# W3's last 64 features done behind W4's row tiles, with W4's sums split 256 and 384

## The chip, the cores and the metric

The kernel runs on one core of one Trainium2 chip. The metric is the device time of one launch in microseconds (us), of the slowest core, which here is the only one. A profile is one execution with every instruction recorded. PE is TensorE, PEld its weight loads, DVE VectorE, ACT ScalarE, SP the engine that issues most of the DMAs.

A timed run scatters by 1 us or more between executions. A trace is far steadier within its loop: the distance between two matmuls of the same program repeats to about 0.01 us. For an effect of some tenths of a us I therefore lean on distances inside the traces, and use the timed runs for the larger effects that I provoke on purpose.

## The reference, cut to what matters

The whole computation mixes a linear attention block and an MLP block over 2048 tokens of 640 features. The change touches only the last part of the MLP block:

```python
x1 = x + hs                                          # 2048 x 640
h2 = _gelu(_layernorm(x1, axis=-1) @ w3) @ w4         # w3: 640 x 1728, w4: 1728 x 640
b  = x1 + h2
return g * a + (1 - g) * b                            # a: attention block, g: gate per token
```

1728 is 13 chunks of 128 features and one rest of 64. That rest is what the change moves.

## The kernel before

The tokens are done in four tiles (`t` = 0 to 3) of 512 tokens (`TS`), each of four chunks of 128 (`cc`). PSUM, where the matmuls leave their sums, is handed out by the kernel in four "pairs" of two banks of 512 float32 columns, and there is no fifth pair.

The rest of 64 features uses the array in halves. In W3 only 64 of its 128 columns are needed, so two matmuls, each for half of the tile's tokens (`LT` = 256), run side by side: "column tiles", 128 rows by 64 columns. In W4 only 64 of its 128 rows are needed, so two matmuls for two chunks of tokens run side by side: "row tiles", 64 by 128. Everything else in this loop uses the array whole ("full").

```python
    def w3_unit(t, i):                       # two chunks of features into one PSUM pair
        ...                                  # cut: h2 and lnT (transposed LayerNorm) of the tile
        pt = pair()
        for k in range(2):
            fc = 2 * i + k
            if fc < FF:                      # FF = 13 full chunks
                for dc in range(DC):
                    nc.tensor.matmul(pt[:, k, :], lhsT=w3_sb[:, dc, fc * P:(fc + 1) * P], rhs=lnT[:, dc, :], ...)
            else:                            # the rest: column tiles
                for dc in range(DC):
                    for v in range(2):
                        nc.tensor.matmul(pt[FR * v:FR * (v + 1), k, 0:LT], lhsT=w3_sb[:, dc, FF * P:F],
                                         rhs=lnT[:, dc, v * LT:(v + 1) * LT], ...)
        ...                                  # cut: GELU on ScalarE, PSUM -> h2

    def w4_tile(t):
        pts = {cc: pair() for cc in (0, 2)}
        for cc in (0, 2):
            ...                              # cut: x1_scale of the next tile (ScalarE)
            for hf in range(2):              # two halves of the 640 outputs
                w4_mm(t, cc, pts, hf, True)  # 13 matmuls
        for cc in (1, 3):
            pts[cc] = pair()
        w4_rest(t, pts)                      # row tiles: end chunks 0 and 2, begin 1 and 3
        for cc in (0, 2):
            w4_out(t, cc, pts[cc])           # VectorE: * (1 - g) + x1, then the store
        last = t == NT - 1
        for cc, hf in ((3, 0), (1, 0), (1, 1), (3, 1)) if last else ((1, 0), (1, 1), (3, 0), (3, 1)):
            ...                              # cut
            w4_mm(t, cc, pts, hf, False)
            ...                              # cut: output of the piece

    for t in range(NT):                      # the loop
        for i in range(NW3):                 # 7 units of W3, with W2 of t + 1 and attention of t between them
            w3_unit(t, i)
            ...                              # cut: w2_unit(t + 1, i), att_unit(t, i - 2)
        if t + 1 < NT:
            ...                              # cut: ln2_rstd
            for cc in range(CPT):
                ln2_apply(t + 1, cc)         # LayerNorm of t + 1 and its DMA transpose into lnT
        w4_tile(t)
```

So in each tile PE goes from full to column tiles (end of W3), to full (W4's first half), to row tiles, and to full again (W4's second half): four changes of the array's shape.

## Time and profile before

| | before |
|---|---|
| time, median of the first 3 runs | 266.99 us (266.32 to 267.23) |
| span of the profile | 265.1 us |
| PE busy | 259.4 us, 98% |
| DVE, ACT, POOL busy | 53%, 32%, 8% |
| granted TensorE clock | 0.997 |

These are the first part of the page (busy us, share of the span, instructions) and the head of its fourth part (the chain of waits that ended last, by engine):

```profile
PE 259.4 (98%) x1728; PEld 162.0 (61%) x1744; DVE 139.3 (53%) x270; ACT 84.2 (32%) x122; POOL 20.3 (8%) x55
...
PE 95%; DMA 1%; ACT 1%; issue 0%; ACTq 0%; DVE 0%
```

PE sets the time. A busy PE is no proof of a full one, though: matmul records overlap (a 320-column matmul is recorded with 0.30 us but the next starts 0.136 us later), so a gap of 0.1 us between two groups is covered by the records and counts as busy. It shows only in the starts. This is PE's timeline of before at the end of W3 and through W4 in tile 1 (start, length, engine, line, operation, tile of the array, shape, how many):

```profile
168.69 1.24 PE L459 MATMUL pp<-lnxT,w_sb 128*128 128x512 bf16 x5
169.86 0.74 PE L464 MATMUL pp<-lnxT,w_sb 128*64 128x256 bf16 x10
170.53 7.24 PE L476 MATMUL pp<-w_sb,h 128*128 128x320 bf16 x52
177.70 0.72 PE L485 MATMUL pp<-w_sb,h 64*128 64x320 bf16 x8
178.35 0.45 PE L476 MATMUL pp<-w_sb,h 128*128 128x320 bf16 x2
```

L464 are the column tiles and L485 the row tiles. (Here and in later views the last line can be cut off by the window that was asked for: all 26 or 52 matmuls of W4 follow.) Five matmuls of 512 columns at the steady 0.216 us would end their stream at 169.77; the column tiles start at 169.86, 0.09 us later. Ten column tiles in pairs of 0.109 us take 0.55 us, to 170.41; W4 starts at 170.53, 0.12 us later. Fifty-two matmuls at 0.1358 us take 7.06 us, to 177.59; the row tiles start 0.11 us later. Four pairs of row tiles take 0.54 us; W4 goes on 0.11 us later. Each change of shape leaves about 0.1 us in which PE streams nothing.

The tail of before, DVE at the end of tile 3. L501 is the last arithmetic of the kernel, on the last 320 columns:

```profile
259.53 0.88 DVE L492 SCALAR_TENSOR_TENSOR oc<-pp,omg,x 128x640 bf16<-128x640 f32 x1 [2.32 <-PE pp L476]
261.29 0.55 DVE L501 SCALAR_TENSOR_TENSOR oc<-pp,omg,x 128x320 bf16<-128x320 f32 x1 [0.88 <-PE pp L476]
```

### The profile page before, as it was taken

To read this page: it belongs to the slowest core of one execution; us is meant where nothing else is said; L and a number is where in the kernel's file an instruction comes from. 1 tells how busy PE (TensorE), PEld (TensorE's weight loads), DVE (VectorE), ACT (ScalarE), POOL (GpSimd) and SP (SyncE) were. 2 spreads that over 40 slices of the span, in tenths; PEclk is the share of its full clock that TensorE was granted. 3 is DMA by queue.
4 is the path that set the end of the run, shared out by engine and by line. 5 is a ranking of instruction groups with operands and counts; after the bars stand their busy time and mean duration, and the time that the engine had idled before them with its cause. 6 is when DMAs were issued, how large, how long until landed. Compare 5 with 4: busy or idle time off the path is not lost.

```text
span 265.1 us, 4244 instructions
## 1 busy us (share of the span) xinstructions
PE 259.4 (98%) x1728; PEld 162.0 (61%) x1744; DVE 139.3 (53%) x270; ACT 84.2 (32%) x122; POOL 20.3 (8%) x55
## 2 busy tenths in 40 slices
PE   8999999999999999999999999999999999999994
PEld 4667555788755644565666556567556567455662
DVE  1688688899858588955422364512464503122032
ACT  1555544321165636522510313430212340333100
POOL 7100010012300140001000001000001000000000
PEclk9999999999999999999999999999999999999998
DMA  7999987015663527500132000132000042000011
GB/s 195 181 212 370 377 242 298 0 40 122 127 97 64 78 51 193 205 0 2 29 70 77 25 0 2 21 78 77 25 0 2 1 99 77 25 0 2 0 62 37
DMA packets 46092, 23.61 MB, mean 89 GB/s; under 512 B 35450, under 2 KB 45434, under 8 KB 46074
## 3 DMA queue, kind: packets, MB, share of 16 engines
q1 hardware_dynamic: 45632, 22.86, 33.2%
q10 hardware_dynamic: 442, 0.49, 0.5%
q8 instruction: 13, 0.21, 0.4%
q14 instruction: 5, 0.04, 0.1%
HBM read 12.21 MB, written 2.62 MB: 56 GB/s over the span
## 4 chain that ended last, share of the span: by engine, by line
PE 95%; DMA 1%; ACT 1%; issue 0%; ACTq 0%; DVE 0%
PE pp L476 22%; PE pp L459 21%; PE pp L307 8%; PE pp L412 8%; PE pp L443 8%; PE pp L190 8%; PE pp L341 8%; PE pp L232 8%; DMA wk_sb<-in_A_wqkv_dram 1%; PE pp L464 1%; PE pp L485 1%; ACT m_sb L381 1%; PE pp L360 1%; PE pp L247 0%; PE pp L379 0%
## 5 line engine op out<-in xcount | busy, mean ns | idle before, releaser
L467 ACT ACTIVATE h<-pp 128x1024 bf16<-128x1024 f32 (+1 forms) x28 | 27.8, 992 | 102.8 <-PE pp L459 94.4
L459 PE MATMUL pp<-lnxT,w_sb 128*128 128x512 bf16 x249 | 59.8, 379 | 0.6
L476 PE MATMUL pp<-w_sb,h 128*128 128x320 bf16 x416 | 57.9, 299 | 0.0
L476 PEld LDWEIGHTS <-h 128*128 128x128 bf16 x416 | 40.0, 98 | 17.0 <-issue 1.9
L459 PEld LDWEIGHTS <-w_sb 128*128 128x128 bf16 x260 | 25.4, 98 | 26.7
L492 DVE SCALAR_TENSOR_TENSOR oc<-pp,omg,x 128x640 bf16<-128x640 f32 x15 | 12.9, 882 | 44.1 <-PE pp L485 27.1
L446 DVE SCALAR_TENSOR_TENSOR x<-pp,gate,x 128x640 f32<-128x640 f32 x16 | 13.9, 868 | 29.4 <-PE pp L443 29.4
L415 DVE TENSOR_TENSOR x<-pp,x_sb 128x640 f32<-128x640 f32 x16 | 13.1, 820 | 22.6 <-PE pp L412 22.6
L182 ACT ACTIVATE e<-pp 128x640 bf16<-128x640 f32 (+1 forms) x26 | 21.5, 826 | 9.6 <-PE pp L232 9.6
L443 PE MATMUL pp<-m_sb,pqT 128*128 128x320 bf16 x160 | 24.3, 299 | 0.0
L412 PE MATMUL pp<-w_sb,hsT 128*128 128x320 bf16 x160 | 23.9, 299 | 0.1
L190 PE MATMUL pp<-wk_sb,xT 128*128 128x320 bf16 (+1 forms) x160 | 22.7, 300 | 0.1
L307 PE MATMUL pp<-x_sb,pk 128*128 128x320 bf16 (+1 forms) x160 | 22.3, 300 | 0.0
L232 PE MATMUL pp<-xT,hsT 128*128 128x512 bf16 x98 | 21.6, 379 | 0.1
L307 PEld LDWEIGHTS <-pk 128*128 128x128 bf16 x160 | 18.8, 117 | 3.5
L412 PEld LDWEIGHTS <-hsT 128*128 128x128 bf16 x160 | 15.6, 98 | 8.2 <-issue 0.2
L443 PEld LDWEIGHTS <-pqT 128*128 128x128 bf16 x160 | 15.7, 98 | 7.7
L190 PEld LDWEIGHTS <-xT 128*128 128x128 bf16 x160 | 15.4, 98 | 6.6 <-DMA xT<-in_A_x_dram 0.6
L341 PE MATMUL pp<-lnxT,w_sb 128*128 128x512 bf16 x77 | 17.8, 379 | 0.2
L232 PEld LDWEIGHTS <-hsT 128*128 128x128 bf16 x100 | 11.8, 118 | 9.7
L277 POOL TENSOR_SCALAR rstd<-mv 128x4 f32<-128x4 f32 (+1 forms) x11 | 3.4, 312 | 156.5 <-DVE mv L283 156.5
L184 DVE SCALAR_TENSOR_TENSOR pk<-pp,e 128x640 bf16<-128x640 f32 x16 | 13.2, 824 | 1.7
(76 smaller groups left out, 189.7 us busy)
## 6 DMA issues: line engine op xcount, KB each, us to landing
out_dram<-oc SPq DMA_DIRECT2D x15, 160.0 KB, 1.8
w_sb<-in_B_w_dram SPq DMA_DIRECT2D x1, 2160.0 KB, 8.4
w_sb<-in_B_w_dram SPq DMA_DIRECT2D x1, 2080.0 KB, 10.2
x_sb<-in_A_x_dram SPq DMA_DIRECT2D x2, 640.0 KB, 10.0
x_sb<-in_A_x_dram SPq DMA_DIRECT2D x1, 1120.0 KB, 7.5
wo_sb<-in_A_wo_dram SPq DMA_DIRECT2D x6, 160.0 KB, 7.7
hsT<-in_A_wqkv_dram SPq DMA_DIRECT2D x1, 800.0 KB, 5.0
m_sb<-in_A_wqkv_dram SPq DMA_DIRECT2D x1, 800.0 KB, 11.1
```

Of the source, the lines that this page charges most:

```text
L182: nc.scalar.activation(ev, src, ACT.Exp)
L184: nc.vector.scalar_tensor_tensor(dst, src, 0.0, ev, op0=ALU.max, op1=ALU.add)
L190: nc.tensor.matmul(pt[:, hf, 0:n], lhsT=xT[:, dc, c * P:(c + 1) * P], rhs=wk_sb[:, dc, hf * HD:hf * HD + n], start=(dc == 0), stop=(dc == ...
L232: nc.tensor.matmul(pt[:, t % 2, :], lhsT=wq_sb[:, dc, :].rearrange("p (m j) -> p j m", j=DC)[:, j], rhs=xT[:, dc, t * TS:(t + 1) * TS], st ...
L307: nc.tensor.matmul(pt[:, hf, 0:HD + hf], lhsT=w, rhs=x_sb[:, c, hf * HD:(hf + 1) * HD + hf], start=(c == 0), stop=(c == NCH - 1))
L341: nc.tensor.matmul(pt[:, i, :], lhsT=w, rhs=lnxT[t][:, dc, :], start=(dc == 0), stop=(dc == DC - 1))
L412: nc.tensor.matmul(pt[:, hf, 0:HD], lhsT=hsT[:, fc, 2 + c * P:2 + (c + 1) * P], rhs=w2_sb[:, fc, hf * HD:(hf + 1) * HD], start=(fc == 0), ...
L443: nc.tensor.matmul(pt[:, hf, 0:HD], lhsT=pqT[:, j, c * P:(c + 1) * P], rhs=m_sb[:, j, hf * HD:(hf + 1) * HD], start=(j == 0), stop=(j == D ...
L446: nc.vector.scalar_tensor_tensor(x1, pt[:, :, 0:HD], gate[:, c:c + 1], x1, op0=ALU.mult, op1=ALU.add)
L459: nc.tensor.matmul(pt[:, k, :], lhsT=w3_sb[:, dc, fc * P:(fc + 1) * P], rhs=lnT[:, dc, :], start=(dc == 0), stop=(dc == DC - 1))
L467: nc.scalar.activation(h2[:, 2 * i * TS:2 * i * TS + n], pt[:].rearrange("p h e -> p (h e)")[:, 0:n], ACT.Gelu_apprx_tanh)
L476: nc.tensor.matmul(dst, lhsT=st[t]["h2"][:, fc * TS + cc * P:fc * TS + (cc + 1) * P], rhs=w4_sb[:, fc, a:b], start=start and fc == 0, stop ...
```

## The change

The intent: do the column tiles of the *next* tile of tokens right behind the row tiles of this one, so that PE goes full, row, column, full, and the column tiles no longer need a visit of their own. They need PSUM columns for that, and all four pairs are taken by W4. So W4's 640 sums are cut into 256 and 384: 256 in the upper half of a pair's first bank and 384 in its second bank, which leaves 256 columns free in the first. In the last tile the pieces are put in an order that leaves a 256-column piece for last.

```diff
+    h2x_p = ctx.enter_context(tc.tile_pool(name="h2x_p", bufs=2))
 ...                                     # w3_unit: the else branch with the column tiles is gone
+    def w3_rest(t, dst):
+        for dc in range(DC):
+            for v in range(2):
+                nc.tensor.matmul(dst[FR * v:FR * (v + 1), :], lhsT=w3_sb[:, dc, FF * P:F],
+                                 rhs=st[t]["lnT"][:, dc, v * LT:(v + 1) * LT], start=(dc == 0), stop=(dc == DC - 1))
+        st[t]["h2x"] = h2x_p.tile([P, LT], BF16, name="h2x")
+        nc.scalar.activation(st[t]["h2x"][:], dst, ACT.Gelu_apprx_tanh)
+
     def w4_dst(cc, pts, hf):
-        return pts[cc][:, hf, 0:HD], hf * HD, (hf + 1) * HD
+        return (pts[cc][:, 0, TS - LT:TS], 0, LT) if hf == 0 else (pts[cc][:, 1, 0:D - LT], LT, D)
 ...                                     # w4_rest reads h2x; w4_out reads 640 columns in a row
         w4_rest(t, pts)
+        if t + 1 < NT:
+            w3_rest(t + 1, pts[0][:, 0, 0:LT])
         for cc in (0, 2):
             w4_out(t, cc, pts[cc])
         last = t == NT - 1
-        for cc, hf in ((3, 0), (1, 0), (1, 1), (3, 1)) if last else ((1, 0), (1, 1), (3, 0), (3, 1)):
+        for cc, hf in ((3, 1), (1, 0), (1, 1), (3, 0)) if last else ((1, 0), (1, 1), (3, 0), (3, 1)):
 ...
+        if t == 0:
+            w3_rest(0, pair()[:, 0, 0:LT])
         w4_tile(t)
```

Only tile 0 still visits column tiles by itself. The number of changes of shape in the loop falls from 4 x 4 = 16 to 5 + 3 + 3 + 2 = 13.

More of the change, by code (lines that the diff above doesn't have):

```diff
@@ L450, in w3_unit @@
     def w3_unit(t, i):
-        if "h2" not in st[t]:
-            st[t]["h2"] = h2p.tile([P, FF * TS + LT], BF16, name="h2")
+        if i == 0:
+            st[t]["h2"] = h2p.tile([P, FF * TS], BF16, name="h2")
         h2, lnT = st[t]["h2"], st[t]["lnT"]
         pt = pair()
-        for k in range(2):
+        n = min(2, FF - 2 * i)
+        for k in range(n):
             fc = 2 * i + k
-            if fc < FF:
-                for dc in range(DC):
-                    nc.tensor.matmul(pt[:, k, :], lhsT=w3_sb[:, dc, fc * P:(fc + 1) * P], rhs=lnT[:, dc, :],
-                                     start=(dc == 0), stop=(dc == DC - 1))
-            else:
-                for dc in range(DC):
-                    for v in range(2):
-                        nc.tensor.matmul(pt[FR * v:FR * (v + 1), k, 0:LT], lhsT=w3_sb[:, dc, FF * P:F],
-                                         rhs=lnT[:, dc, v * LT:(v + 1) * LT], start=(dc == 0), stop=(dc == DC - 1))
-        n = 2 * TS if 2 * i + 1 < FF else TS + LT
-        nc.scalar.activation(h2[:, 2 * i * TS:2 * i * TS + n], pt[:].rearrange("p h e -> p (h e)")[:, 0:n],
-                             ACT.Gelu_apprx_tanh)
+            for dc in range(DC):
+                nc.tensor.matmul(pt[:, k, :], lhsT=w3_sb[:, dc, fc * P:(fc + 1) * P], rhs=lnT[:, dc, :],
+                                 start=(dc == 0), stop=(dc == DC - 1))
+        nc.scalar.activation(h2[:, 2 * i * TS:(2 * i + n) * TS], pt[:].rearrange("p h e -> p (h e)")[:, 0:n * TS],
+                             ACT.Gelu_apprx_tanh)
+    def w3_rest(t, dst):
+        for dc in range(DC):
+            for v in range(2):
[3 more added lines that the diff above has]
+        nc.scalar.activation(st[t]["h2x"][:], dst, ACT.Gelu_apprx_tanh)
     def w4_dst(cc, pts, hf):
-        return pts[cc][:, hf, 0:HD], hf * HD, (hf + 1) * HD
+        return (pts[cc][:, 0, TS - LT:TS], 0, LT) if hf == 0 else (pts[cc][:, 1, 0:D - LT], LT, D)
     def w4_mm(t, cc, pts, hf, start):
@@ L484, in w4_rest @@
                     dst, a, b = w4_dst(u + 2 * v, pts, hf)
-                    nc.tensor.matmul(dst, lhsT=st[t]["h2"][rows, FF * TS + u * P:FF * TS + (u + 1) * P],
+                    nc.tensor.matmul(dst, lhsT=st[t]["h2x"][rows, u * P:(u + 1) * P],
                                      rhs=w4_sb[rows, FF, a:b], start=u == 1, stop=u == 0)
@@ L491, in w4_out @@
         oc = outp.tile([P, D], BF16, name="oc")
-        nc.vector.scalar_tensor_tensor(oc[:].rearrange("p (h e) -> p h e", h=2), pt[:, :, 0:HD],
-                                       omg[:, c:c + 1], x1[:].rearrange("p (h e) -> p h e", h=2),
-                                       op0=ALU.mult, op1=ALU.add)
+        nc.vector.scalar_tensor_tensor(oc[:], pt[:].rearrange("p h e -> p (h e)")[:, TS - LT:TS - LT + D],
+                                       omg[:, c:c + 1], x1[:], op0=ALU.mult, op1=ALU.add)
         nc.sync.dma_start(out2[c * P:(c + 1) * P, :], oc[:])
```

## The prediction

> **What bounds the kernel.** TensorE: the page has PE busy 98% of 265.1 us, the run's core list a granted clock of 0.997, the chain of waits 95% PE. VectorE (53%) and ScalarE (32%) are slack. Only what changes PE's stream, or makes it wait, counts.
>
> **PE's stream.** The matmul columns stay the same: W4 streams 640 columns per contraction, cut 320+320 or 256+384. PE's timeline has 52 matmuls of 320 columns in about 7.06 us (135.8 ns each); I estimate 109 ns for 256 and 163 ns for 384 columns, the same sum. Weight loads shouldn't limit 109 ns: the timeline shows 30 matmuls of 120 and 40 columns, each with its own load, in 1.53 us, 51 ns each.
>
> Removed are switches of the array's tiling. The Trainium skill, "TensorEngine Tiling (Array Packing)", Key Properties, says that changing the tiling mode drains TensorE. The trace agrees and gives the size. From the starts in PE's timeline of tile 0, beyond the steady pace: full to column tiles (129.21 to 129.31 us) 0.10 us, column to full 0.12, full to row 0.11, row to full 0.11. Before, each of four tiles pays all four: 16 switches. After, tiles 0 to 2 go full, row, column, full, and only tile 0 still visits column tiles by itself: 13 switches. PE saves three times 0.1 us, 0.3 us, all critical.
>
> **New waits?** The moved matmuls need the next tile's transposed LayerNorm. In tile 0 its four transposes are issued from 129.88 to about 133.8 us and land 2.6 us later, the last at about 136.4. The moved matmuls would start at about 137.0 (in tiles 1 and 2 W4 starts 0.7 us earlier against them than now). Margin 0.6 us: no wait. The GELU of feature chunk 13 shrinks from 768 to 512 columns, to about 0.6 us (1.02 us for 1024, 0.81 for 768), and is needed 12 matmuls of 109 ns after W4 starts: margin 0.4 us.
>
> The moved sums share a PSUM bank with W4's finished sums of chunk 0. The Trainium skill, "PSUM — Partial Sum Buffer", PSUM bank collisions, says that two engines must not use one bank at once, so I expect VectorE's output step of chunk 0 to start after the new GELU, about 1 us later than now; no run yet shows this. The buffer is next needed some 7 us later, so it is free, as are the extra GELUs (0.4 us each) on ScalarE.
>
> **The tail.** The last piece has 256 columns instead of 320: VectorE's last operation falls from 0.55 to about 0.48 us (slope from 0.88 us for 640), and the last store is smaller. About 0.1 us, critical.
>
> **Sum.** 266.99 - 0.3 - 0.1 = 266.6 us; the runs of before spread 0.9 us, so this is barely visible. Range 265.8 to 267.3. Faster by over 2%: 0.01; within 2%: 0.97; slower: 0.02.
>
> **What would show it.** PE's timeline after: W4's first half directly behind W3 in tiles 1 to 3; one gap of about 0.1 us between row and column tiles; W4's widths at about 109 and 163 ns; no idle of PE's weight loads put down to a transpose or a GELU.
>
> **What would make it wrong.** Transposes landing after W4's row tiles (some tenths of a us, three times); 256-column matmuls paced by their weight loads (10 ns each would cost 2 us over 208); the framework making matmuls wait for whole PSUM tiles; a lower granted clock.

## The result, and the profile after

After takes 266.59 us, the median of 6 runs (266.17 to 266.91), beside 267.11 us of before (6 runs, 266.32 to 267.86). The ratio is 0.9981, with a 95% interval of 0.9961 to 1.0. (Ratios here are the mean time of one kernel's fast runs over that of the other's of the same rounds, so not quite the ratio of the medians.) I ran after once more, beside new runs of before; that is the run `after_again`:

> The changed kernel once more, unaltered, beside before on one chip, for a narrower interval. Theory (3 switches of 0.1 us and 0.1 to 0.2 us of tail): 0.4 to 0.5 us under before, ratio about 0.9983; stretch between the W4 starts of tiles 0 and 3 115.92 us again; from W4's start in tile 3 to the end of VectorE's last operation 15.56 us again. If the ratio is 1.000 with an interval that leaves 0.9983 out, the gain that the trace shows inside the loop is given back elsewhere.

It took 266.65 us (6 runs) beside 266.99 us (11 runs), ratio 0.9972, interval 0.9948 to 0.9997. The two intervals together say that after is faster by something between 0 and 0.5%. They can't say by which part of the change; the traces can.

PE's timeline after, in tile 1 as above (L479 is W4, L488 the row tiles, L468 the column tiles, now of tile 2):

```profile
169.15 1.24 PE L460 MATMUL pp<-lnxT,w_sb 128*128 128x512 bf16 x5
170.23 7.23 PE L479 MATMUL pp<-w_sb,h 128*128 128x256 bf16 x52
177.39 0.72 PE L488 MATMUL pp<-w_sb,h2x 64*128 64x256 bf16 x8
178.03 0.74 PE L468 MATMUL pp<-lnxT,w_sb 128*64 128x256 bf16 x10
178.70 0.50 PE L479 MATMUL pp<-w_sb,h 128*128 128x256 bf16 x3
```

W4 starts 1.08 us after W3's last five matmuls, which is 5 x 0.216 with nothing between. The row tiles start 7.16 us after W4's first half began, before 7.17: the new widths stream as fast as the old. Row tiles to column tiles take 0.64 us, of it 0.54 for the four pairs, so this change of shape costs about 0.10 us, one switch and not two. From W3's last five matmuls to W4's second half the same work takes 178.70 - 169.15 = 9.55 us after and 178.35 - 168.69 = 9.66 us before: 0.11 us less.

From W4's first matmul in tile 0 to W4's first matmul in tile 3, the distance that I call the stretch, the saving has come three times: 246.20 - 129.98 = 116.22 us before, 245.69 - 129.77 = 115.92 us after. The second trace of after gives 115.91. These are the four lines, first of before, then of after:

```profile
129.98 7.24 PE L476 MATMUL pp<-w_sb,h 128*128 128x320 bf16 x52
246.20 7.24 PE L476 MATMUL pp<-w_sb,h 128*128 128x320 bf16 x52
```

```profile
129.77 7.24 PE L479 MATMUL pp<-w_sb,h 128*128 128x256 bf16 x52
245.69 7.23 PE L479 MATMUL pp<-w_sb,h 128*128 128x256 bf16 x52
```

No new wait came with it. The longest waits of PE's weight loads after (engine, line, what for: us in total, times, longest) name no transpose and no GELU in this loop:

```profile
PEld L202 <- issue: 2.6, 8, 0.8
PEld L488 <- issue: 1.3, 4, 0.3
PEld L468 <- issue: 1.2, 4, 0.4
PEld L479 <- issue: 1.1, 5, 0.3
PEld L190 <- DMA xT<-in_A_x_dram: 0.6, 2, 0.4
```

The first and the last of these lines belong to the start of the kernel. The three between are the loads behind a change of shape, which were not pulled ahead of it here. Their times, 4 + 4 + 5 = 13, are the number of switches; the same view of before has 8 + 4 + 4 = 16.

The tail after:

```profile
259.35 0.89 DVE L495 SCALAR_TENSOR_TENSOR oc<-pp,omg,x 128x640 bf16<-128x640 f32 x1 [2.60 <-PE pp L479]
260.77 0.48 DVE L503 SCALAR_TENSOR_TENSOR oc<-pp,omg,x 128x256 bf16<-128x256 f32 x1 [0.53 <-PE pp L479]
```

From W4's start in tile 3 to the end of DVE's last operation, 261.84 - 246.20 = 15.64 us have become 261.25 - 245.69 = 15.56 us, 0.08 us less, nearly all of it the operation on fewer columns.

The profiled spans differ by 0.7 us (265.1 and 264.4). Of that, 0.30 us is the stretch, 0.08 us the tail's arithmetic, about 0.1 us lies behind DVE's last operation, where the last store lands (see old_tail), and 0.21 us lies before W4's first matmul in tile 0, where the number of switches is the same. The last part is not the change's: `after_again`, the same program, has its W4 start at 130.28 and not at 129.77.

### The profile page after: what moved, and what is told of

Same layout as the page of the kernel before. It is cut to its first block, busy times and chain, and to the rows that moved or that the text cites. A ratio compares the mean times of both kernels' runs of the same rounds, so it can differ in the third digit from the quotient of the medians.

```text
span 264.4 us, 4255 instructions
## 1 busy us (share of the span) xinstructions
PE 259.7 (98%) x1744; PEld 162.2 (61%) x1744; DVE 139.3 (53%) x270; ACT 85.1 (32%) x126; POOL 20.2 (8%) x55
## 4 chain that ended last, share of the span: by engine, by line
PE 91%; SPq 3%; DMA 3%; ACT 1%; issue 0%; DVE 0%
PE pp L479 22%; PE pp L460 21%; PE pp L307 8%; PE pp L413 8%; PE pp L444 8%; PE pp L341 8%; PE pp L232 8%; PE pp L190 4%; SPq L121 3%; DMA xT<-in_A_x_dram 3%; PE pp L468 1%; PE pp L488 1%; ACT m_sb L381 1%; PE pp L360 1%; PE pp L247 0%; SPq L124 0%
## 5 line engine op out<-in xcount | busy, mean ns | idle before, releaser
L479 PE MATMUL pp<-w_sb,h 128*128 128x256 bf16 (+1 forms) x416 | 57.9, 299 | 0.0
L462 ACT ACTIVATE h<-pp 128x1024 bf16<-128x1024 f32 (+1 forms) x28 | 26.9, 961 | 82.2 <-PE pp L460 82.2
L479 PEld LDWEIGHTS <-h 128*128 128x128 bf16 x416 | 40.3, 98 | 16.6 <-issue 1.1
```

The lines of the kernel that those rows point to most:

```text
L462: nc.scalar.activation(h2[:, 2 * i * TS:(2 * i + n) * TS], pt[:].rearrange("p h e -> p (h e)")[:, 0:n * TS], ACT.Gelu_apprx_tanh)
L479: nc.tensor.matmul(dst, lhsT=st[t]["h2"][:, fc * TS + cc * P:fc * TS + (cc + 1) * P], rhs=w4_sb[:, fc, a:b], start=start and fc == 0, stop ...
```

## The experiments

My theory: the gain in the loop is three switches of the array's shape, about 0.1 us each. The rivals: the new split of W4's sums is the gain (A), or a loss that hides more gain (B); it helps to take the 64 features off W3's last unit, wherever they go (C); a switch costs next to nothing (D); row to column costs two switches (E); or there are changes off the critical path that count after all (F, G).

The table collects what was measured. "Stretch" is W4's start in tile 0 to W4's start in tile 3; "tail" is W4's start in tile 3 to the end of DVE's last operation; both from the trace. Four kernels ran beside 11 runs of before with a median of 267.09 us, four others beside 11 with 267.13 us.

| kernel | switches | stretch | tail | median us | ratio to before (95%) |
|---|---|---|---|---|---|
| before | 16 | 116.22 | 15.64 | 267.11 | 1 |
| after | 13 | 115.92 | 15.56 | 266.59 | 0.9981 (0.9961 to 1.0) |
| after_again | 13 | 115.91 | 15.56 | 266.65 | 0.9972 (0.9948 to 0.9997) |
| split_only | 16 | 116.22 | 15.72 | 267.25 | 1.0006 (0.999 to 1.0022) |
| own_visit | 16 | 116.23 | 15.56 | 266.80 | 0.999 (0.9975 to 1.0005) |
| col_full_alt | 48 | 118.95 | 15.64 | 270.62 | 1.0133 (1.0117 to 1.0149) |
| row_col_alt | 31 | 117.95 | 15.57 | 268.44 | 1.0052 (1.0038 to 1.0066) |
| rest_in_chunk2 | 13 | 115.91 | 15.56 | 266.72 | 0.9984 (0.9972 to 0.9996) |
| old_tail | 13 | 115.91 | 15.71 | 266.86 | 0.9988 (0.9975 to 1.0002) |
| merged_first | 11 | see text | 15.57 | 266.55 | 0.9977 (0.9965 to 0.9989) |
| early_rest | 16 | 130.45 | 15.56 | 280.66 (1 run) | - |

All results were correct.

### split_only: the split of the sums alone

```diff
 # before, with
     def w4_dst(cc, pts, hf):
-        return pts[cc][:, hf, 0:HD], hf * HD, (hf + 1) * HD
+        return (pts[cc][:, 0, TS - LT:TS], 0, LT) if hf == 0 else (pts[cc][:, 1, 0:D - LT], LT, D)
 # and w4_out reading 640 columns in a row, as in after; nothing else
```

> Before, with W4's sums split 256 and 384 and the joined output step, and nothing else; the last tile keeps its order, so the last piece has 384 columns. Theory (the gain is fewer tiling switches): the switches stay at 16, so the stretch from W4's first matmul in tile 0 to W4's first matmul in tile 3 stays at 116.22 us as before (not 115.92 as after), W4's 52 matmuls still take 7.06 us, and the tail gets about 0.07 us longer; about 267.2 us, ratio to before 1.000. Rival A (the split itself is the gain): the stretch shrinks to about 115.9 us. Rival B (256-column matmuls are paced by their weight loads): W4's halves get longer by 10 ns a narrow matmul, 0.26 us a half.

The stretch stayed at 246.67 - 130.45 = 116.22 us, equal to before's. W4's first half and the switch behind it still took 7.17 us. The tail grew by 0.08 us, as the last piece has 384 columns. Rivals A and B fall: the split neither gains nor costs anything in the loop. It is only what makes room.

### own_visit: the same work away from the row tiles

```diff
 # after, with
         w4_rest(t, pts)
-        if t + 1 < NT:
-            w3_rest(t + 1, pts[0][:, 0, 0:LT])
 ...
             w4_mm(t, cc, pts, hf, False)
+            if t + 1 < NT and (cc, hf) == (1, 1):
+                w3_rest(t + 1, pts[0][:, 0, 0:LT])
```

> After, with the next tile's 64 features done behind W4's pieces of chunk 1, away from the row tiles, so that they visit column tiles by themselves: 16 switches again. Theory: the stretch from W4's start in tile 0 to W4's start in tile 3 returns to about 116.2 us (before 116.22, after 115.92), total about 0.3 us over after. Rival C (taking the 64 features off the last W3 unit is what helps, by a shorter GELU or a freer PSUM pair, wherever they go): the stretch stays at 115.9 us.

PE's timeline of own_visit in tile 1, with the column tiles (L468) between two quarters of W4:

```profile
178.05 0.72 PE L488 MATMUL pp<-w_sb,h2x 64*128 64x256 bf16 x8
178.70 3.71 PE L479 MATMUL pp<-w_sb,h 128*128 128x256 bf16 x26
182.34 0.74 PE L468 MATMUL pp<-lnxT,w_sb 128*64 128x256 bf16 x10
183.01 1.16 PE L479 MATMUL pp<-w_sb,h 128*128 128x256 bf16 x9
```

The stretch is back at 116.23 us; the whole saving of the loop is gone, with everything else of the change kept. Rival C falls: it is the place right behind the row tiles that counts. The timed run (0.999) can't tell this kernel from after or from before.

### col_full_alt: 32 more switches on purpose

```diff
 # before, W3's last unit: full and column matmuls take turns (cut: the old loop skips this unit)
+        for dc in range(DC if 2 * i + 1 == FF else 0):
+            nc.tensor.matmul(pt[:, 0, :], lhsT=w3_sb[:, dc, 2 * i * P:(2 * i + 1) * P], rhs=lnT[:, dc, :], ...)
+            for v in range(2):
+                nc.tensor.matmul(pt[FR * v:FR * (v + 1), 1, 0:LT], lhsT=w3_sb[:, dc, FF * P:F],
+                                 rhs=lnT[:, dc, v * LT:(v + 1) * LT], ...)
```

> Before, with the last W3 unit's 5 full matmuls and its 5 pairs of column tiles taking turns: the same matmuls, but 10 switches a tile in place of 2 there, 32 more in all. Theory (each switch costs 0.10 to 0.12 us of PE): 3.2 to 3.8 us longer, of it 2.4 to 2.9 us in the stretch from W4's start in tile 0 to that in tile 3 (3 tiles, 24 switches); about 270.6 us, ratio 1.013. Rival D (a switch costs next to nothing, the 0.3 us is chance or something else): within 0.5 us of before.

PE's timeline of col_full_alt in tile 0, the first two of five turns:

```profile
128.36 0.38 PE L456 MATMUL pp<-lnxT,w_sb 128*128 128x512 bf16 x1
128.67 0.30 PE L459 MATMUL pp<-lnxT,w_sb 128*64 128x256 bf16 x2
128.90 0.39 PE L456 MATMUL pp<-lnxT,w_sb 128*128 128x512 bf16 x1
129.22 0.30 PE L459 MATMUL pp<-lnxT,w_sb 128*64 128x256 bf16 x2
```

A full matmul of 512 columns takes 0.31 to 0.32 us here in place of 0.216, a pair of column tiles 0.23 in place of 0.109: 0.10 us into column tiles and 0.12 out of them. The stretch grew by 118.95 - 116.22 = 2.73 us for 24 switches, 0.114 us each, and the whole kernel by 270.62 - 267.09 = 3.53 us for 32, 0.110 each. Rival D falls, here by timed runs too.

### row_col_alt: is row to column one switch or two?

```diff
 # after, w4_rest and w3_rest taking turns in tiles 0 to 2 (the tile's h2x is read by the row tiles as in after)
         for n, (u, hf) in enumerate(((0, 0), (0, 1), (1, 0), (1, 1))):
             for v in range(2):
                 ...                                  # one pair of row tiles; x: the free columns of chunk 0's pair
+            if t + 1 < NT:
+                w3_rest_mm(t + 1, x, n)              # one pair of column tiles
+        if t + 1 < NT:
+            w3_rest_mm(t + 1, x, DC - 1)
+            w3_rest_act(t + 1, x)                    # its GELU
```

> After, with the four pairs of row tiles and the five pairs of column tiles taking turns in tiles 0 to 2: 9 switches in place of 3 in each visit, 18 more in all, every one between row and column tiles. Theory (a row-to-column switch costs one switch like any other, 0.10 to 0.12 us, which is why the change gains): 1.8 to 2.2 us longer than after, about 268.6 us, all of it in the three visits. Rival E (a direct change between row and column tiles costs two switches, and the gain has another source): 3.6 to 4.3 us longer. Rival D: no difference.

PE's timeline of row_col_alt in tile 0 (L494 row tiles, L467 column tiles):

```profile
137.02 0.28 PE L494 MATMUL pp<-w_sb,h2x 64*128 64x256 bf16 x2
137.23 0.30 PE L467 MATMUL pp<-lnxT,w_sb 128*64 128x256 bf16 x2
137.46 0.34 PE L494 MATMUL pp<-w_sb,h2x 64*128 64x384 bf16 x2
137.73 0.30 PE L467 MATMUL pp<-lnxT,w_sb 128*64 128x256 bf16 x2
```

A pair of 256 columns takes 0.21 us before a change from row to column and 0.23 before one from column to row: 0.10 and 0.12 us over its stream of 0.109. The stretch is 117.95 - 115.92 = 2.03 us longer than after's for 18 switches, 0.113 each; the runs give 1.8 us (268.44 against 266.65, from different rounds and chips). Rival E falls. A direct change between row and column tiles costs what any other change does, and that is what the kernel's change lives on: two shapes side by side need three switches, apart they need four.

### early_rest: when do the transposes land?

After shows no wait for the transposes, so their margin can't be read from it. This kernel asks for them too early.

```diff
 # after, with the pairs of chunks 1 and 3 taken before W4's first half, and
             for hf in range(2):
                 w4_mm(t, cc, pts, hf, True)
+            if cc == 0 and t + 1 < NT:
+                w3_rest(t + 1, pts[1][:, 0, 0:LT])
 # in place of the call behind w4_rest
```

> After, with the next tile's 64 features done 3.5 us earlier, behind W4 of chunk 0, into PSUM columns of chunk 1: to measure when the transposes really land, as no wait shows it in after. My estimate from the issue times and 2.6 us to landing: the last lands at about 6.5 us after the first transpose is issued, so PE must stand still before the moved matmuls for about 2.9 us in tile 0 and 3.6 us in tiles 1 and 2, until some 0.6 us before the moment at which after starts them; with two more switches a tile about 277 us in all. If PE starts them later than after does against the first issue, the margin I claimed is not there; if PE hardly waits, the transposes land early and the margin is large.

PE's timeline of early_rest in tile 1 (behind the last two: idle before, and what ended it):

```profile
173.11 3.69 PE L479 MATMUL pp<-w_sb,h 128*128 128x256 bf16 x26
177.72 0.30 PE L468 MATMUL pp<-lnxT,w_sb 128*64 128x256 bf16 x1 [0.91 <-DMA lnxT<-ln]
180.36 1.27 PE L468 MATMUL pp<-lnxT,w_sb 128*64 128x256 bf16 x9 [2.34 <-DMA lnxT<-ln]
181.56 5.85 PE L479 MATMUL pp<-w_sb,h 128*128 128x256 bf16 x26
```

The transposes are issued from 173.77 in this tile, and the last has landed by 180.36, 6.59 us later (6.57 in tile 0, 6.56 in tile 2). In after the moved matmuls start 7.91, 7.14 and 7.15 us after the first issue in tiles 0, 1 and 2. So the margin is 0.55 to 0.6 us in tiles 1 and 2, as expected, and 1.3 us in tile 0, where W4 starts later against the transposes because tile 0 keeps its own column visit.

The expectation says two more switches a tile, which is a miscount: it is one more (full, column, full, row, full), 16 in all. The total was a miss too: 280.66 us where I had expected about 277. The trace shows where the time went. The waits themselves had the expected size (2.8, 3.6 and 3.6 us from the moment at which PE would have gone on, 0.1 us after the last streamed column of W4). The rest, some 4 us, is a lower granted clock behind the waits of tiles 1 and 2. From the windows of early_rest (stretch of time, its length, busy time and instructions of PE, PEld, DVE, ACT and POOL, then the granted clock, the DMA share and GB/s):

```profile
133.40:136.20 2.80, 0.33 (x4) 0.12 (x3) 0.00 (x0) 0.00 (x0) 0.00 (x0) 1.00 0.59 117
...
180.36:185.80 5.44, 5.44 (x27) 3.42 (x28) 0.00 (x0) 2.53 (x4) 0.00 (x0) 0.50 0.00 0
186.00:187.30 1.30, 1.30 (x9) 0.64 (x7) 0.00 (x0) 0.00 (x0) 0.00 (x0) 1.00 0.00 0
```

After the wait in tile 0 the clock stayed at 1.00; after the longer one in tile 1 it was 0.50 for 5.4 us of full work, so those 26 W4 matmuls took 5.85 us in the records and not 3.7 (4.64 in tile 2). The longest unbroken idle of PE was 2.34 or 2.35 us in all three tiles; tiles 1 and 2 had 0.9 us of it more just before, with one matmul between. The Trainium skill, "TensorE: Matmul & The Clock Gate", Part 1, says that the clock falls to half after an idle window of some 3.4 us, and that these windows run free of the kernel. The length agrees: cut finely, the clock of this trace was at half from 179.16 to 185.99 us and from 226.95 to 230.36, that is for 6.83 and 3.41 us. But no idle of 3.4 us was needed here: in the 3.4 us before 179.16 PE had still worked for about 1 us, and then run the one matmul. The trace also shows how much depends on the margin of 0.6 us that the change leaves: in tiles 1 and 2 a late transpose cost more than its own wait.

### rest_in_chunk2: the late output step of chunk 0

```diff
 # after, with
-            w3_rest(t + 1, pts[0][:, 0, 0:LT])
+            w3_rest(t + 1, pts[2][:, 0, 0:LT])
```

> After, with the moved sums in the free columns of chunk 2's PSUM pair in place of chunk 0's. If VectorE's output step of chunk 0 is late only because its bank is shared with the moved sums, it starts about 1.2 us earlier in tiles 0 to 2, right behind the row tiles, and chunk 2's waits for the GELU instead. Theory (that delay is off the critical path): stretch between the W4 starts of tiles 0 and 3 115.9 us as in after, total 266.6 us. Rival F (the late output step costs time): faster than after, stretch under 115.8 us.

DVE's two output steps behind the row tiles of tile 0, first in after, then in rest_in_chunk2 (start, length, ..., how many, idle before, and what ended it):

```profile
138.78 1.68 DVE L495 SCALAR_TENSOR_TENSOR oc<-pp,omg,x 128x640 bf16<-128x640 f32 x2 [7.61 <-ACT h2x L471]
```

```profile
138.39 0.88 DVE L495 SCALAR_TENSOR_TENSOR oc<-pp,omg,x 128x640 bf16<-128x640 f32 x1 [6.24 <-PE pp L488]
139.75 0.88 DVE L495 SCALAR_TENSOR_TENSOR oc<-pp,omg,x 128x640 bf16<-128x640 f32 x1 [0.48 <-ACT h2x L471]
```

This is the same step in before, behind the row tiles:

```profile
137.63 1.68 DVE L492 SCALAR_TENSOR_TENSOR oc<-pp,omg,x 128x640 bf16<-128x640 f32 x2 [6.25 <-PE pp L485]
```

In after the first output step waits for the new GELU and starts 138.78 - 129.77 = 9.01 us after W4; in before it is 137.63 - 129.98 = 7.65. With the sums in chunk 2's bank it is 138.39 - 130.74 = 7.65 again, and the second step waits in its place. So it is the shared place in PSUM that makes it late: the kernel keeps ScalarE and VectorE apart although their columns differ. The Trainium skill, "PSUM — Partial Sum Buffer", PSUM bank collisions, leads one to expect this for a shared bank. This run moves the sums to another pair, so it doesn't tell the bank from the whole pair, and merged_first below speaks for the pair. The stretch is 115.91 us either way. The delay of 1.36 us is real and costs nothing; rival F falls.

### old_tail: the order of the last pieces

```diff
 # after, with
-        for cc, hf in ((3, 1), (1, 0), (1, 1), (3, 0)) if last else ...
+        for cc, hf in ((3, 0), (1, 0), (1, 1), (3, 1)) if last else ...
```

> After, with the last tile's pieces in the order of before, so that the last piece has 384 columns and not 256. Theory: the stretch between the W4 starts of tiles 0 and 3 stays at 115.9 us; VectorE's last operation takes 0.62 us and not 0.48, and from W4's start in tile 3 to that operation's end it is about 15.70 us (before 15.64, after 15.56). Total about 0.15 to 0.2 us over after. Rival G (the tail gives nothing, the store's landing hides it): the span from W4's start in tile 3 to the end is as in after.

The stretch is as in after. The last operation, on 384 columns, takes 0.62 us, and the tail is 261.99 - 246.28 = 15.71 us: 0.15 more than after, 0.07 more than before. Both sizes are as expected. What the smaller last store gives stays open: from the end of DVE's last operation to the end of the span there are 3.15 us in both traces of after, 3.26 in before and 3.31 here, but 3.21 in split_only with the same 384 columns, 3.18 to 3.23 in the other four fast runs that end on 256 columns and 3.20 in col_full_alt with 320, and spans are read to 0.1 us. By the timed runs (0.9988 against 0.9972 to 0.9984 for the kernels with the new order) rival G can't be excluded; by the trace, the end of the arithmetic at least comes earlier.

### merged_first: a try at 11 switches

```diff
 # after, with tile 0's own visit gone, and
+        if t == 0:
+            w3_rest(0, pts[1][:, 0, 0:LT])
+            w3_rest(1, pts[3][:, 0, 0:LT])
         w4_rest(t, pts)                  # its last pair of row tiles writes the banks that the GELUs read
-        if t + 1 < NT:
+        if 0 < t < NT - 1:
             w3_rest(t + 1, pts[0][:, 0, 0:LT])
```

> A try at a better version: after, with tile 0's own visit to column tiles joined to the next one: in tile 0 W4's first half, then column tiles for tiles 0 and 1, then the row tiles, 11 switches in place of 13. Theory: from the first matmul of W3's last unit in tile 0 to W4's start in tile 3 (after 117.76 us) two switches less, 0.22 us, minus at most 0.1 to 0.2 us where the row tiles wait for the GELU of tile 0's features: 117.5 to 117.75 us; total 266.4 to 266.6 us. If the GELU is waited for longer than the switches were worth, it is slower than after.

From the first matmul of W3's last unit in tile 0 to W4's start in tile 3 it took 246.35 - 128.57 = 117.78 us, after 245.69 - 127.93 = 117.76. The expected gain did not come. PE's weight loads of merged_first in tile 0 show where it stayed:

```profile
138.02 0.22 PEld L488 LDWEIGHTS <-h2x 64*128 64x128 bf16 x6 [0.20 <-ACT h2x L471]
138.57 0.10 PEld L488 LDWEIGHTS <-h2x 64*128 64x128 bf16 x2 [0.33 <-issue]
138.92 0.33 PEld L479 LDWEIGHTS <-h 128*128 128x128 bf16 x4 [0.26 <-issue]
```

The row tiles begin on time, but their last pair is loaded 0.33 us after the six loads before it. The view calls this wait "issue", but the records of the matmuls say more: in the third pair one matmul starts at 138.31 and the other, which writes chunk 3, only at 138.57 and with a wait on ScalarE's semaphore. The second GELU ran from 138.13 to 138.51 and read chunk 3's first bank; this matmul writes the second bank of the same pair. So it waited for a GELU with which it shares the pair and no bank, though no run takes the GELU away. The two switches saved, 0.22 us, are spent on this 0.26 us. The timed runs (266.55 us, 0.9977) don't tell it from after. It is no better version.

## Why the prediction was right

The prediction was 266.6 us, and after took 266.59. With runs that scatter by 0.7 us, a hit to 0.01 us is luck; what can be judged is each step.

- **PE sets the time, and W4's columns stream alike in both cuts.** Right: split_only has the stretch of before to 0.01 us. The 256-column matmuls are not held up by their weight loads.
- **A switch costs 0.10 to 0.12 us, and three fewer save 0.3 us.** Right: the stretch fell by 0.30 us; 24 added switches of one kind cost 0.114 us each and 18 of another 0.113. The saving vanished when the column tiles were put elsewhere.
- **Row to column is one switch.** Assumed in the prediction from the skill's sentence that a change of mode drains, and shown by row_col_alt; that it is a drain which costs the time is not shown.
- **No new wait.** Right. The margin before the transposes was claimed as 0.6 us: it is 0.55 to 0.6 us in tiles 1 and 2. For tile 0 the prediction named that number too, mixing tile 0's issue times with the earlier start of the later tiles; there it is 1.3 us. The margin of chunk 13's GELU was put at 0.4 us; in tile 1 that GELU ends at 171.03 and the matmul that needs it would start at 170.23 + 12 x 0.109 = 171.54, so 0.5 us.
- **Chunk 0's output step starts later, for free.** Right in kind and too small in size: 1.36 us, put at about 1.
- **The tail gives 0.1 us.** The arithmetic gives 0.08 us. The share of the store is not settled.

The timed runs alone would not have shown any of this: both intervals of after nearly touch 1.

## What to carry to other kernels

Where small matmuls use the array in halves, put all visits to row and column tiles next to each other: each change of shape costs PE about 0.11 us here, whichever two shapes it lies between, and it hides inside "busy" because matmul records overlap. Read it from the starts of the matmuls, beyond their steady pace. When an effect is a tenth of a per cent, judge it by distances inside the trace and by a run that multiplies the suspected cost (32 switches more, 3.5 us), and find the margin of a wait that doesn't show by asking for the data too early.

## What the Trainium skill lacked or had wrong

- "TensorEngine Tiling (Array Packing)", Key Properties, says that changing the tiling mode drains TensorE, but gives no cost. Here a switch cost 0.10 to 0.12 us from start to start (0.114 us over 24 full/column switches, 0.113 us over 18 row/column switches), and a direct change between row and column tiles cost one switch, not two.
- "TensorE: Matmul & The Clock Gate", LDWEIGHTS, gives columns / 1.2 as nanoseconds of a load, 107 ns for 128 columns. Loads of 128 columns are recorded with 95 to 99 ns in most groups here, but loads of 64 columns (the column tiles) with 106 to 110 ns, about twice what the formula gives for them. Nor is the formula a pace: 30 matmuls of 120 and 40 columns, each with its own load of 128, started within 1.53 us in before, 51 ns each. That comes near the factor of about 2 that the same page measures for its Fast Weight Load, so it is the formula alone that misleads.
- The same page, Part 1, says that an idle window of some 3.4 us halves the clock and that some 3.4 us of sustained work bring it back. The windows agree: in early_rest the clock was at half for 6.83 and 3.41 us, two windows and one, and work took 5.6 us in tile 1 and 3.2 us in tile 2 to bring it back. What is too strict is the idle window: the clock fell at 179.16 us although PE had worked for about 1 us of the 3.4 us before.
- "PSUM — Partial Sum Buffer" tells to keep engines apart by bank and quadrant of partitions, or simply by bank, but no page says what keeping them apart does to a schedule: here it moved one output step by 1.36 us, at no cost, and in merged_first it held a row tile for 0.26 us although only the pair was shared, not the bank.
